# Four edits to a kernel with a planned order: idle products between the first sums, a split first piece, high words first, remainder first

## The chip, the cores and the metric

The kernel runs on one NeuronCore of a Trainium2 chip. The metric is device time in microseconds of one execution. The engines of the core are named PE (TensorE; PEld is its weight load), DVE (VectorE), ACT (ScalarE), POOL (GpSimd) and SP (SyncE, which here issues nearly all transfers). Each engine works through its own list of instructions in the order in which they were written, and an instruction waits for semaphores of the others.

## The reference, cut to what matters

For 2048 positions of 576 channels, a gate mixes two branches:

```python
x = A_u
g = sigmoid((x * gate_w).sum(-1, keepdims=True))
a = _A_ref(x, A_re, A_im, B_re, B_im, C_re, C_im, log_dt, Dskip)   # long convolution
b = _B_ref(x, w_q, k1, k2, u, v)                                   # 4096 experts
return g * a + (1 - g) * b
```

Branch A builds a filter of 2048 taps for each channel, K = Re(sum over 128 states of C exp(dt A l) dt B), and convolves each channel with it (in the reference by FFT); `u * Dskip` is added. Branch B projects every position with `w_q` to 32 heads of two halves, scores each half against 64 keys (`s1 = q1 k1^T`, `s2 = q2 k2^T`), takes the two best of each, the two best of their four sums, a softmax over these two, and forms

```python
act = gelu(einsum("nd,nhkd->nhk", xf, u[top_e]))
out = einsum("nhk,nhk,nhkd->nd", g, act, v[top_e])
```

with `u` and `v` of 4096 rows (the experts).

## The kernel before, in words

**What is multiplied.** No expert row is gathered. All 2048 x 4096 products of positions and expert rows (`a`), all scores against keys folded with `w_q` (`s`), and the output product with a sparse weight matrix (`o`) are dense matmuls. For precision each f32 operand is scaled by a power of two and split into two f16 words, a high one (`hi = f16(s*x)`) and a low one (`s*x - hi`). A product of two operands is then three matmuls: high by high, high by low, low by high. The 576 channels are four pieces of 128 and a remainder of 64, in which high and low word share the 128 rows. `triple` (L943 on) writes one such group: twelve matmuls of 512 columns for the four pieces and two for the remainder (`wrem`).

**Stages.** First the start: the inputs come in, x is read in four blocks of 512 positions (`x_load`, `x_first`, `x_build`), the expert rows u in eight blocks of 512 (`u_load`, `u_build`). For each operand a scale is needed first: ACT squares the values and sums them along the row (`accum_out`, which adds a short ACTIVATION_READ_ACCUMULATOR), PE adds these sums over the partitions with a matrix of ones (`onesb`; bank `sq`), and DVE makes a power of two of the result in four one-column operations (`root_scale`). For the first blocks of x and u, `scale_first` does this in four parts, the remainder and PARTS (two pieces, one, one), as the transfers land, and each part has its own sum matmul of one column into `sq`. `x_norm` forms the squared norms of the 512 positions in a bank `x`; for the first block it first writes six products of 512 columns whose result is not used, waits until u's sums are written, and then writes the five real ones.

The second stage, up to about 678 us, mixes `s` and `a` groups with the making of the filter (`kP`, `kb` matmuls with much work on ACT, DVE and POOL) and the position transform of x, the first stage of the convolution's forward transform (`u_stage1`, bank `u`, 16 steps). The third does the rest of the convolution's transforms (`k`, `pr`/`pi`, `pv`) beside the other `s` groups and the last `a` groups. The last, from about 991 us, takes the 16 tiles of 128 positions one after the other in the sequence ORDER: one-hot matrices that DVE builds by comparison (`onehot`: A, Be, Bg), 256 small one-hot products a tile that scatter the gate weights (bank `S`, in two groups, q = 0 and q = 2), a multiplication on DVE that empties the banks into `gl`, the split into `wh` (high and low words), and then 192 matmuls `o` with the expert rows `v`.

**What sets the order.** The program is generated by Python coroutines. Each engine has a modelled free time, and PE's is the planner's clock: `mm` puts it forward by columns/2400 + 0.003 us for each matmul. A coroutine yields until its inputs are ready by this model (`ready`, with `late` as an extra delay) or a buffer is free (`need`, `take`, `free`), and is called again at that modelled time; the main loop then writes the next `s` or `a` group. What comes out is one fixed order for each engine; on the chip only semaphores hold an instruction back, and one that waits holds all that is behind it on its engine. PSUM has eight banks of [128, 512] f32, given out under quotas (`sc`, `wb`, `kb`).

**Lines that the steps touch.** `mm` L205-L214 (all matmuls carry L214, all DVE, ACT and POOL operations L134, all transfers L205), `squares` L445, `x_norm` L463, `x_first` L481, `scale_first` L503, `u_stage1` L1074, `onehot` L1497, `prep` L1510, `u_load` L1320, `u_build` L1335, and the main loop from L1743. In `u_stage1` a step has two column halves (hh, 288 columns each), two frequency rows (g, on 64 rows of the array each) and three products (z, w): z picks the high or low word of the table `tu`, w that of the data `uh`, whose high word ACT writes and whose low word DVE writes.

Of the kernel before, what the change touches and what calls it, by code (L numbers as in the profile page):

```python
# [17 lines left out]
AF = mybir.ActivationFunctionType  # L18
# [120 lines left out]
def body(ctx: ExitStack, tc: tile.TileContext, xT, au, par, logdt, dskip, gatew, wq, kT, uT, vv,  # L139
# [196 lines left out]
    def newcol(again=False):  # L336

        col[again] += 1
        c = 96 + col[1] % 96 if again else col[0]
        return slice(c, c + 1)  # L340

    def short(c0, n):

        return sc[:, c0:c0 + n].bitcast(BF16)[:, 1:2 * n:2]
# [100 lines left out]
    def squares(a, r, sq, dst):  # L445

        acc = newcol(), newcol()
        S.activation(sq[:, 0:4, :], a, AF.Square, accum_out=sc[:, acc[0]])
        S.activation(sq[:, 4, :], r, AF.Square, accum_out=sc[:, acc[1]])
        yield from ready(sq)  # L450
        tag = side()
        yield from need(tag)
        p = bank(tag, "sq")
        mm(p[:, 0:2], onesb, short(acc[0].start, 2), True, True, 0.05)
        yield from ready(p)
        V.tensor_reduce(out=dst, in_=p[:, 0:2], axis=AX, op=OP.add)
        free(tag, dst)

    marks = {"x": [], "s": [], "h": [], "u": []}
    first_u = [None, None]  # L460
    ahead, normed = [], []

    def x_norm(tb, sq):  # L463

        yield from need("kb")
        p = bank("kb", f"x{tb}")
        if tb == 0:
            for k in range(6):
                mm(p, onesb, sq[:, k % 4, :], True, True)
            while not marks["s"]:  # L470
                yield 0.1
        for k in range(5):
            mm(p, onesb, sq[:, k, :], k == 0, k == 4)
        normed.append(tb)
        yield from ready(p)
        while tb == 0 and 1 not in scaled:
            yield 0.3
        V.tensor_reduce(out=nx[:, tb:tb + 1], in_=p, axis=AX, op=OP.max)
        free("kb", nx)
# [23 lines left out]
    def scale_first(a, r, sq, keep=None):  # L503

        acc = [newcol() for _ in range(1 + len(PARTS))]
        if keep is None:
            V.memset(sq[64:128, 4], 0.0)
        V.memset(sc[64:128, acc[0]], 0.0)
        yield from ready(r)
        S.activation(sq[0:64, 4], r[0:64], AF.Square, accum_out=sc[0:64, acc[0]])  # L510
        V.tensor_copy(r[64:128], r[0:64])
        for n, (m, w) in enumerate(PARTS):
            yield from ready(a[:, m:m + w])
            S.activation(sq[:, m:m + w], a[:, m:m + w], AF.Square, accum_out=sc[:, acc[n + 1]])
        yield from ready(sq)
        yield from need("kb")
        p = bank("kb", "sq")
        for n, c in enumerate(acc):
            mm(p[:, 0:1], onesb, short(c.start, 1), n == 0, n == len(PARTS), 0.05)
        yield from ready(p)  # L520
        out = root_scale(p[:, 0:1], 1.02)
        if keep is not None:
            V.tensor_copy(keep, p[:, 0:1])
        free("kb", out[0])
        return out
# [548 lines left out]
    def u_stage1():  # L1074
        nonlocal uf
        yield from need("slot")
        us = slot([4, D], F32, "us")
        columns.add(us.tensor.name)
        s_u, i_u = root_scale(nx2, 1.02)
        ended = [0]  # L1080
        ld = {}

        def load(p):
            a = us[:, p % 2, :]
            for g in range(2):
                l, far = U_PAIRS[2 * p + g]
                dma(a[64 * g:64 * g + 64], bass.AP(tensor=au.tensor, offset=au.offset + l * D,
                                                   ap=[[64 * D, R1], [(far - l) * D, 2], [1, D]]))
            tu = uf.tile([128, 2, 128], F16, tag="tu", name=f"tu{p}", bufs=2)
            dma(tu, tu_d[:, p])  # L1090
            ld[p] = a, tu

        def tail(p, tag, pbs):
            for g in range(2):
                o = us[:, 2 + g, :]
                for hh in range(2):
                    pb = pbs[hh][g]
                    yield from ready(pb)
                    ov = o[:, 288 * hh:288 * hh + 288]
                    S.activation(ov, pb[:, :288], AF.Copy)  # L1100
                    free(tag, ov)
                yield from ready(ov)
                dma(pair_rows(su_d, 2 * p + g), o)
            ended[0] += 1

        load(0)
        for p in range(NT):
            a, tu = ld.pop(p)
            yield from ready(a, tu)
            while ended[0] < p - 1:  # L1110
                yield 0.3
            h = uf.tile([128, 2, D], F16, tag="uh", name=f"uh{p}", bufs=2)
            S.activation(h[:, 0], a, AF.Copy, scale=s_u)
            yield from ready(h)
            V.scalar_tensor_tensor(h[:, 1], a, s_u, h[:, 0], op0=OP.mult, op1=OP.subtract)
            if p + 1 < NT:
                load(p + 1)
            yield from ready(h)
            while ended[0] < p:
                yield 0.3  # L1120
            tag = side()
            hungry[0] = p * NCK < 17 * kdone[0]
            yield from need(tag, 4)
            hungry[0] = False
            pbs = [[bank(tag, f"u1_{p}_{g}_{hh}") for g in range(2)] for hh in range(2)]
            for hh in range(2):
                cs = slice(288 * hh, 288 * hh + 288)
                for n, (z, w) in enumerate(((0, 0), (0, 1), (1, 0))):
                    for g in range(2):
                        r = slice(64 * g, 64 * g + 64)  # L1130
                        mm(pbs[hh][g][:, :288], tu[r, z], h[r, w, cs], n == 0, n == 2, 0.063)
            spawn(tail(p, tag, pbs))
            del pbs
            yield 12
        while ended[0] < NT:
            yield 1
        free("slot")
        quota(raw=2)
        while not kstored[0]:
            yield 1  # L1140
        V.scalar_tensor_tensor(iuk, iuk, 2.0 ** -28, i_u, op0=OP.mult, op1=OP.mult)
        UF.__exit__(None, None, None)
        uf = 0
# [176 lines left out]
    def u_load(c):  # L1320
        a = slot([4, 512], F32, f"us{c}")
        r = actp.tile([128, 512], F32, tag="ur", name=f"ur{c}")
        cs = slice(512 * c, 512 * c + 512)
        if c:
            dma(a, uT[0:512, cs].rearrange("(k p) n -> p k n", p=128))
        dma(r[0:64], uT[512:576, cs])
        if c:
            dma(r[64:128], uT[512:576, cs])
        else:
            halves_load(a, uT, cs)  # L1330
        return a, r
# [3 lines left out]
    def u_build(c):  # L1335
# [23 lines left out]
        rem = wrems[c % 2]  # L1359
        if c == 0:  # L1360
            for k in range(4):
                S.activation(hl[:, 0, k, :], a[:, k, :], AF.Copy, scale=s)
                marks["h"].append(S.free + 0.28)
            S.activation(rem[:, 0, :], r, AF.Copy, scale=s)
            marks["h"].append(S.free + 0.28)
# [144 lines left out]
    def prep(t):  # L1510
# [17 lines left out]
                yield 0.3  # L1528
            oh = {q: onehot(t, q) for q in range(3)}
        for q in (0, 2):  # L1530
            yield from ready(*oh[q], *oh[q + 1], late=2.5 if t in ORDER[:3] else 0.0)
            yield from need("wb", 4)
            pbs = []
            for d in (q, q + 1):
                A, Bg = oh.pop(d)
                both = [bank("wb", f"S{t}_{d}_{r}") for r in range(2)]
                for j in range(16):
                    for z in range(2):
                        for r, pS in enumerate(both):
                            rows = slice(64 * r, 64 * r + 64)  # L1540
                            mm(pS[:, 32 * j:32 * j + 32], A[rows, j // 2, :, j % 2], Bg[rows, z, j // 2, :, j % 2],
                               z == 0, z == 1, 0.014)
                pbs.append((16 * d, both))
                del both, pS
            if q == 0:
                oh[3] = onehot(t, 3)
            for n0, both in pbs:
                for r, pS in enumerate(both):
                    yield from ready(pS)
                    pv = pS.rearrange("p (k b) -> p b k", b=32)  # L1550
                    for h in range(2):
                        gv = gl[h].rearrange("p b (r n) -> p b r n", r=2)[:, :, r, n0:n0 + 16]
                        V.tensor_tensor(out=gv, in0=pv[:, 16 * h:16 * h + 16], in1=gv, op=OP.mult)
                    free("wb", *gl)
            del pbs, pS, pv, both
# [311 lines left out]
```

## Time and profile before

| | |
|---|---|
| median of 3 runs | 1441.61 us |
| lowest, highest | 1441.29, 1444.52 us |
| profiled execution, its time | 1442.26 us |
| profiled execution, span from first to last instruction | 1440.3 us |
| PE busy | 1421.2 us (99%) |
| DVE, ACT, POOL busy | 1161.8, 769.9, 484.2 us |
| granted TensorE clock | 1.000 |
| matmuls | 16151 |

The profile is one execution on the chip. Busy time is time in which at least one instruction of the engine was under way; matmuls are pipelined, so a train of them is shorter than the sum of their durations: a 512-column matmul shows 379 ns in a train, and twelve of them take 2.75 us. In the timeline each row has a start (us from the span's start), a duration, the engine, the operation and its tiles as output<-inputs, and in brackets the idle time before it and what ended it; neighbouring instructions of a kind are merged into one row with their count. In the list of waits a row names the waiting engine and tile, what it waited for, the total, the number of times and the longest. SPq is SP's queue of transfers.

### The profile page before, as it was taken

To read this page: it belongs to the slowest core of one execution; us is meant where nothing else is said; L and a number is where in the kernel's file an instruction comes from. 1 tells how busy PE (TensorE), PEld (TensorE's weight loads), DVE (VectorE), ACT (ScalarE), POOL (GpSimd) and SP (SyncE) were. 2 spreads that over 40 slices of the span, in tenths; PEclk is the share of its full clock that TensorE was granted. 3 is DMA by queue.
4 is the path that set the end of the run, shared out by engine and by line. 5 is a ranking of instruction groups with operands and counts; after the bars stand their busy time and mean duration, and the time that the engine had idled before them with its cause. 6 is when DMAs were issued, how large, how long until landed. Compare 5 with 4: busy or idle time off the path is not lost.

```text
span 1440.3 us, 40769 instructions
## 1 busy us (share of the span) xinstructions
PE 1421.2 (99%) x16151; PEld 835.6 (58%) x16153; DVE 1161.8 (81%) x4595; ACT 769.9 (53%) x1281; POOL 484.2 (34%) x492
## 2 busy tenths in 40 slices
PE   7999999999999999999999999999999999999999
PEld 3444445455455445455555444456787787787785
DVE  6899899879886997875999897689877777877840
ACT  6346876796784876844655655666333223323310
POOL 0325357547356346230547899700000000000000
PEclk9999999999999999999999999999999999999999
DMA  8235323442334323159675677967443332442400
GB/s 302 75 116 165 90 74 121 126 144 72 109 100 154 93 93 115 49 172 308 222 264 191 243 258 271 307 216 249 151 131 130 117 122 95 136 147 69 159 10 17
DMA packets 134239, 215.43 MB, mean 150 GB/s; under 512 B 11040, under 2 KB 79904, under 8 KB 127648
## 3 DMA queue, kind: packets, MB, share of 16 engines
q1 hardware_dynamic: 133952, 212.80, 45.2%
q8 instruction: 127, 2.08, 0.6%
q14 instruction: 64, 0.52, 0.1%
q10 hardware_dynamic: 96, 0.02, 0.0%
HBM read 141.48 MB, written 71.30 MB: 148 GB/s over the span
## 4 chain that ended last, share of the span: by engine, by line
PE 87%; DVE 5%; DMA 1%; issue 0%; ACT 0%; SPq 0%; DVEq 0%
PE o L214 25%; PE s L214 24%; PE a L214 21%; PE S L214 3%; PE kb L214 2%; PE pr L214 2%; PE wb L214 2%; PE pv L214 1%; PE y L214 1%; PE kP L214 1%; PE k L214 1%; PE u L214 1%; DVE vhl L134 1%; DMA wq<-in_wq_dram 1%; DVE gl L134 1%; DVE A L134 1%
## 5 line engine op out<-in xcount | busy, mean ns | idle before, releaser
L214 PE MATMUL o<-vhl,wh 128*128 128x288 f16 (+2 forms) x3072 | 382.7, 286 | 0.0
L214 PE MATMUL s<-whl,xb 128*128 128x512 f16 x1536 | 363.9, 379 | 0.0
L214 PE MATMUL a<-xb,uhl 128*128 128x512 f16 x1536 | 358.8, 379 | 0.5 <-ACT uhl L134 0.3
L214 PEld LDWEIGHTS <-wh 128*128 128x128 f16 x3072 | 292.4, 98 | 84.1 <-issue 3.7
L214 PEld LDWEIGHTS <-xb 128*128 128x128 f16 x1792 | 170.7, 98 | 209.2 <-issue 14.5
L214 PEld LDWEIGHTS <-uhl 128*128 128x128 f16 x1536 | 147.3, 98 | 177.4 <-issue 3.2
L134 DVE FIND_INDEX8 i<-m,s 128x8 uint32<-128x64 f32 x1024 | 206.1, 219 | 0.0
L134 ACT ACTIVATE wh<-gl,s_wg 128x1024 f16<-128x1024 f32 x64 | 69.0, 1137 | 197.5 <-DVE gl L134 197.5
L134 DVE MAX8 m<-s 128x8 f32<-128x64 f32 x1024 | 145.9, 212 | 30.4 <-PE s L214 29.4
L134 POOL TENSOR_TENSOR CS<-CS,ex 128x512 f32<-128x512 f32 x72 | 98.0, 1392 | 147.5 <-DVE ex L134 146.1
L134 DVE TENSOR_TENSOR gl<-S,gl 128x256 f32<-128x256 f32 x256 | 88.4, 413 | 36.8 <-PE S L214 36.8
L134 ACT ACTIVATE go<-a,i_a 128x512 f32<-128x512 f32 x93 | 62.5, 684 | 97.2 <-PE a L214 70.2
L134 POOL TENSOR_TENSOR e<-aN,rt 128x512 f32<-128x512 f32 x72 | 83.2, 1176 | 49.9 <-PE kb L214 43.8
L134 DVE TENSOR_TENSOR A<-iota_a,vals 128x2048 f16<-128x2048 f16 x64 | 77.9, 1217 | 23.3 <-PE S L214 23.3
L134 ACT ACTIVATE gl<-gl 128x1024 f32<-128x1024 f32 x64 | 63.6, 1045 | 45.3 <-DMA gl<-g_d 36.8
L134 DVE SCALAR_TENSOR_TENSOR wh<-gl,s_wg,wh 128x1024 f16<-128x1024 f32 x62 | 77.6, 1279 | 12.4 <-ACT wh L134 12.3
L214 PE MATMUL s<-wrem,xb 128*128 128x512 f16 x256 | 76.2, 379 | 0.0
L214 PE MATMUL a<-xb,wrem 128*128 128x512 f16 x256 | 75.9, 379 | 0.0
L134 DVE MATCH_VALUE_LOAD i<-m,s 128x8 f32 x1024 | 69.4, 68 | 0.1
L134 ACT ACTIVATE CS<-CS 128x1024 f32<-128x1024 f32 x57 | 59.2, 1044 | 7.3 <-DVE CS L134 7.3
L134 POOL TENSOR_TENSOR ex<-ex,gN 128x512 f32<-128x512 f32 x36 | 44.8, 1256 | 53.3 <-ACT ex L134 53.1
L134 DVE SCALAR_TENSOR_TENSOR ya<-o,om,ya 128x288 f32<-128x288 f32 (+2 forms) x32 | 15.1, 512 | 55.4 <-PE o L214 55.4
(209 smaller groups left out, 2098.3 us busy)
## 6 DMA issues: line engine op xcount, KB each, us to landing
g_d<-go SPq DMA_DIRECT2D x128, 256.0 KB, 2.5
gl<-g_d SPq DMA_DIRECT2D x32, 1024.0 KB, 5.5
wq<-in_wq_dram SPq DMA_DIRECT2D x16, 1152.0 KB, 5.6
su_d<-us SPq DMA_DIRECT2D x32, 288.0 KB, 2.6
sk_d<-k1o SPq DMA_DIRECT2D x32, 288.0 KB, 2.7
ui<-su_d SPq DMA_DIRECT2D x16, 576.0 KB, 3.9
ki<-sk_d SPq DMA_DIRECT2D x16, 576.0 KB, 5.5
vn<-in_vv_dram SPq DMA_DIRECT2D x32, 288.0 KB, 5.4
```

The costliest lines, as they stand in the source:

```text
L134: return f(*a, **k)
L214: T.matmul(o, l, r, start=start, stop=stop)
```

## The change

In the start, `scale_first` takes the bank `x0` itself and writes products of 512 columns whose result is not used between its one-column sums: for x four on the remainder's squares ahead of the second sum, one ahead of the third, one ahead of the fourth; for u two ahead of the third sum and one ahead of the fourth, all on x's squares. The six in `x_norm` stay. The first piece of the first expert rows' high words is made by ACT (256 columns) and DVE (256 columns) instead of ACT alone. In the position transform all products with high data words come first, over both column halves, and those with the low words last. For the second and later blocks of expert rows, the two remainder loads are issued before the large load, and the remainder's square is written before the large square. For the first three tiles the one-hot products are written when their matrices are 3.8 us old by the planner's clock, not 2.5.

```diff
     def squares(a, r, sq, dst):
         acc = newcol(), newcol()
+        S.activation(sq[:, 4, :], r, AF.Square, accum_out=sc[:, acc[1]])
         S.activation(sq[:, 0:4, :], a, AF.Square, accum_out=sc[:, acc[0]])
-        S.activation(sq[:, 4, :], r, AF.Square, accum_out=sc[:, acc[1]])
...
+    first_x = []
...
     def x_norm(tb, sq):
-        yield from need("kb")
-        p = bank("kb", f"x{tb}")
+        if tb:
+            yield from need("kb")
+        p = bank("kb", f"x{tb}") if tb else first_x[1]
...
         p = bank("kb", "sq")
+        if keep is None:
+            yield from need("kb")
+            first_x.extend((sq, bank("kb", "x0")))
+        idle_on, over = first_x
+        idle_at = ((), (4,) * 4, (0,), (2,)) if keep is None else ((), (), (0, 1), (2,))
         for n, c in enumerate(acc):
+            for k in idle_at[n]:
+                mm(over, onesb, idle_on[:, k], True, True)
             mm(p[:, 0:1], onesb, short(c.start, 1), n == 0, n == len(PARTS), 0.05)
...
-            for hh in range(2):
-                cs = slice(288 * hh, 288 * hh + 288)
-                for n, (z, w) in enumerate(((0, 0), (0, 1), (1, 0))):
+            for n, (z, w) in enumerate(((0, 0), (1, 0), (0, 1))):
+                for hh in range(2):
+                    cs = slice(288 * hh, 288 * hh + 288)
                     for g in range(2):
                         r = slice(64 * g, 64 * g + 64)
                         mm(pbs[hh][g][:, :288], tu[r, z], h[r, w, cs], n == 0, n == 2, 0.063)
...
-        if c:
-            dma(a, uT[0:512, cs].rearrange("(k p) n -> p k n", p=128))
         dma(r[0:64], uT[512:576, cs])
         if c:
             dma(r[64:128], uT[512:576, cs])
+            dma(a, uT[0:512, cs].rearrange("(k p) n -> p k n", p=128))
         else:
             halves_load(a, uT, cs)
...
             for k in range(4):
-                S.activation(hl[:, 0, k, :], a[:, k, :], AF.Copy, scale=s)
+                w = 512 if k else 256
+                S.activation(hl[:, 0, k, :w], a[:, k, :w], AF.Copy, scale=s)
+                if k == 0:
+                    V.tensor_scalar(hl[:, 0, k, w:], a[:, k, w:], s, None, op0=OP.mult)
                 marks["h"].append(S.free + 0.28)
...
         for q in (0, 2):
-            yield from ready(*oh[q], *oh[q + 1], late=2.5 if t in ORDER[:3] else 0.0)
+            yield from ready(*oh[q], *oh[q + 1], late=3.8 if t in ORDER[:3] else 0.0)
```

## The prediction, made before the result was known

> **What bounds the kernel now.** First the page: the busy shares say which engine the time belongs to.
>
> ```profile
> PE 1421.2 (99%) x16151; PEld 835.6 (58%) x16153; DVE 1161.8 (81%) x4595; ACT 769.9 (53%) x1281; POOL 484.2 (34%) x492
> ```
>
> PE is busy for 1421.2 of the span's 1440.3 us, so only 19.1 us are left in which it has nothing in flight. No other engine can become the bound by a few instructions; an edit is worth something only if it shortens one of PE's waits or adds one. So the second view is the list of what PE waited for, and here it is over the whole span.
>
> ```profile
> PE sq L214 <- ACT xb L134: 8.7, 4, 4.6
> PE u L214 <- DVE uh L134: 2.0, 2, 1.4
> PE kb L214 <- issue: 1.5, 1, 1.5
> PE sq L214 <- ACT uhl L134: 1.4, 2, 1.0
> PE S L214 <- DVE gl L134: 0.7, 2, 0.5
> PE k L214 <- DMA ksb<-k_d: 0.6, 1, 0.6
> ```
>
> The columns are the total, the number of times and the longest. The first row is the start, before any input has arrived. The second is the position transform, the fourth the sums of the expert rows, the fifth the one-hot products: one edit of the change lies at each of them. I went to each in the timeline, the third view, first to the start (start, duration, engine; times are from the span's start).
>
> ```profile
> 4.56 0.16 PE L214 MATMUL sq<-sc,onesb 128*128 128x1 bf16 x1 [4.56 <-ACT xb L134]
> 7.48 0.16 PE L214 MATMUL sq<-sc,onesb 128*128 128x1 bf16 x1 [2.76 <-ACT xb L134]
> 8.09 0.16 PE L214 MATMUL sq<-sc,onesb 128*128 128x1 bf16 x1 [0.45 <-ACT xb L134]
> 9.22 0.16 PE L214 MATMUL sq<-sc,onesb 128*128 128x1 bf16 x1 [0.97 <-ACT xb L134]
> 9.25 2.72 PE L214 MATMUL x<-xb,onesb 128*128 128x512 bf16 x6
> 11.76 0.39 PE L214 MATMUL sq<-sc,onesb 128*128 128x1 bf16 x3
> 12.60 0.16 PE L214 MATMUL sq<-sc,onesb 128*128 128x1 bf16 x1 [0.45 <-ACT uhl L134]
> 12.63 1.24 PE L214 MATMUL x<-xb,onesb 128*128 128x512 bf16 x5
> 14.21 2.76 PE L214 MATMUL a<-xb,uhl 128*128 128x512 f16 x12 [0.35 <-ACT uhl L134]
> ```
>
> These are PE's rows alone. ACT's and DVE's in the same stretch that the edit touches:
>
> ```profile
> 10.18 1.06 ACT L134 ACTIVATE uhl<-us 128x1024 bf16<-128x1024 f32 x1 [0.39 <-DMA us<-in_uT_dram]
> ...
> 11.23 0.61 ACT L134 ACTIVATE uhl<-us 128x512 bf16<-128x512 f32 x1
> ...
> 13.31 0.15 DVE L134 COPY nu<-sq 128x1 f32<-128x1 f32 x1
> 13.38 0.47 DVE L134 TENSOR_SCALAR xb<-xs,sci 128x512 f16<-128x512 f32 x1
> 13.44 2.56 ACT L134 ACTIVATE uhl<-us,sci 128x512 f16<-128x512 f32 x4 [0.89 <-DVE sci L134]
> ```
>
> Up to 12.60 the sums wait for squares, and the squares for inputs. From the last sum the path is: scale on DVE, first high words on ACT, first real product at 14.21. From there PE runs with hardly a gap, so whatever this point moves, the end moves by.
>
> **First high words on two engines.** ACT now makes 256 of the first piece's 512 columns and DVE the rest. Between 1024 and 512 columns ACT's time falls from 1.06 to 0.61, 0.45 for 512 columns, so half a piece saves 0.22 us. DVE's half lies between its 1-column copy (0.15) and its 512-column scaling (0.47); I take the middle, 0.31, so from 13.46 it ends at 13.77, before ACT's half at about 13.92. The first two products read ACT's half, the next two DVE's. The five x products ahead of them, at some 0.22 from 12.63 on, leave the array free from about 13.7. So the first product comes at 13.99: **-0.22 us** (ends 0, if the array is not free, and -0.5, if only those five bound it). DVE's 0.31 pushes all its later work in the start. The cover: the pieces of x it delays come after 16 products of about 0.23 us (2.76 for 12), some 3.7 us. Without that cover it would cost 0.31.
>
> **Idle products.** Nine more products of 512 columns: four, one and one between the four sums of x, two and one between those of u; the six that stood behind x's sums stay. The six took 2.72 us, some 0.42 each after allowing for the longer last one; the five at 12.63 took 1.24, about 0.22 each. So the array doubled its pace somewhere between. At 0.42 each, the four in x's sums take 1.7 us of a gap of 2.76, and the single ones 0.42 of 0.45 and of 0.97: they fit. In u's sums, the three at 0.22 each end at about 12.5, before ACT releases the last sum at 12.60: nothing. At 0.42 each they end at about 13.1 and hold that sum back by 0.48 us. The array has had work since 4.56 by then, much more than before, and had the 0.22 us pace at 12.63 without it; I take **0**, and keep +0.48. There is no gain either: the first real products already ran at 0.23 us each.
>
> [...]
>
> **High words first in the position transform.** The products come in pairs on two halves of the rows.
>
> ```profile
> 96.00 0.30 PE L214 MATMUL u<-uh,tu 64*128 64x288 f16 x2
> 96.91 0.79 PE L214 MATMUL u<-uh,tu 64*128 64x288 f16 x10 [0.62 <-DVE uh L134]
> ...
> 115.22 0.30 PE L214 MATMUL u<-uh,tu 64*128 64x288 f16 x2
> 116.94 0.79 PE L214 MATMUL u<-uh,tu 64*128 64x288 f16 x10 [1.42 <-DVE uh L134]
> ```
>
> One pair runs, then PE waits until DVE has written the low words (`uh`), then ten run. Ten take 0.79 with a last one of 0.30, so a pair costs (0.79 - 0.30)/4 = 0.12. In the new order four pairs need no low words, three more than now: 3 x 0.12 = 0.37 of each wait is filled. Two waits: **-0.73 us** (ends: 0, if the planner puts these steps where DVE is not late, and -0.73). The banks of the first half finish up to 0.25 us later, so ACT's copies do too; they feed a store, and nothing on PE waits for that. No instruction is added.
>
> **Remainder first.** For the second and later expert rows the two remainder loads and their square go ahead of the large one.
>
> ```profile
> 72.62 0.67 SPq L205 DMA_DIRECT2D us<-in_uT_dram  x1
> 73.34 1.50 SPq L205 DMA_DIRECT2D ur<-in_uT_dram  x2
> ...
> 79.18 1.91 ACT L134 ACTIVATE uhl<-us 128x2048 bf16<-128x2048 f32 x1 [2.11 <-DMA us<-in_uT_dram]
> ...
> 81.85 0.16 PE L214 MATMUL sq<-sc,onesb 128*128 128x2 bf16 x1 [0.95 <-ACT uhl L134]
> ...
> DMA to landing us min/median/max: 5.8/6.1/6.3
> ```
>
> The last row is that of the remainder's loads in this stretch. ACT waits for the large load (79.18), squares it, then the remainder (0.61, as the same shape took at 11.23), then the sum can run, 2.67 us after the landing. With the remainder done in ACT's idle time this would be 2.06. But the second remainder load was issued at about 74.25 and landed near 80.05, right behind the large one: they land in order of issue. Put last, the large load lands near 80.05, and the sum runs at 82.1 instead of 81.85: **+0.2 us**. If the large load landed when it does now, it would be 0.6 sooner; if the issue of two more loads ahead of it also leaves the wire idle for as long as they take on it (80.05 - 79.18 = 0.87), 1.1 later. On SP the three issues take as long in either order, so nothing behind them is held. For the six later expert rows the list of PE's waits has no entry: nothing.
>
> **Later one-hot products.** For the first three tiles they are emitted 1.3 us later on the planner's clock.
>
> ```profile
> 996.26 1.77 PE L214 MATMUL S<-Bg,A 64*128 64x32 f16 x128
> ...
> 1006.88 0.97 PE L214 MATMUL S<-Bg,A 64*128 64x32 f16 x64
> 1007.29 1.41 DVE L134 TENSOR_TENSOR gl<-S,gl 128x256 f32<-128x256 f32 x4
> ...
> 1008.10 0.19 PE L214 MATMUL S<-Bg,A 64*128 64x32 f16 x1 [0.25 <-DVE gl L134]
> ...
> 1008.76 0.96 PE L214 MATMUL S<-Bg,A 64*128 64x32 f16 x63 [0.47 <-DVE gl L134]
> ```
>
> The third tile's second group takes 2.84 us from first to last (1006.88 to 1009.72) where the one before takes 1.77: 1.07 lost while DVE, four evictions from 1007.29 to 1008.70, gives back banks. Started 1.3 later, at 1008.2, its first half ends at 1009.1, behind the last eviction: **-1.07 us** (ends -1.07 and 0). PE has other products to run meanwhile. Queued behind those groups are DVE's evictions and splits, which the output products of the tile read; the list of PE's waits has no row for output products, so this is covered now, and would cost up to 1.3 a group if it were not.
>
> **The sum** is -0.22 + 0 - 0.73 + 0.2 - 1.07 = -1.8 us. The profiled execution took 1442.26 us (span 1440.3, 2.0 around it), 0.65 above the median of 1441.61. So the sum gives 1440.4 for such an execution and **1439.8** as a median. All good ends together give -2.9 (1438.7), all bad ones (0.48 and 1.1) +1.6 (1443.2).
>
> **The rivals.** What the parts do not hold is the order. The planner counts 0.216 us for each 512-column product, so nine of them put its clock forward by about 2 us in the start, where the chip has idle time. Everything planned behind it, the mixture of a, s and kb products above all, falls out somewhat differently.
>
> *The redrawn order gives the gain back* (0.27). The waits above are accidents of one order: two out of sixteen transform steps, one sum out of seven. Another order can have as many elsewhere; one new wait like the 1.5 of kb or the 1.42 at 116.94 takes most of the sum, two take all. Time 1441.6, with one more such wait 1443.1. Against it: the one-hot wait lies among output products, behind the mixture, where little is left to be redrawn.
>
> *It removes others too* (0.12). Without the waits of kb (1.5), sq (1.0 more) and k (0.6), 3.1 us more go: 1436.7. Nothing in the edits aims at them.
>
> *The array keeps its 0.42 us pace through u's sums* (0.07): if work in bursts with pauses of 0.5 to 1 us between them does not bring the 0.22 us pace by 12.6, the idle products cost their 0.48, and the gain is 1.3: 1440.3. Against it: in this execution the pace had changed by 12.63 with less work before it. [...]
>
> *Slower: the hand-over at 650 to 680 runs dry* (0.09). There PE lives on products of the expert rows while the filter's last blocks are written and read back.
>
> ```profile
> 652.16 2.75 PE L214 MATMUL a<-xb,uhl 128*128 128x512 f16 x12
> ...
> 679.11 1.39 PE L214 MATMUL k<-ksb,tk 128*128 128x288 f16 x10 [0.58 <-DMA ksb<-k_d]
> ```
>
> The cover was already 0.58 us short. A group is these twelve products and two remainders, fourteen at 0.216 (2.75 for twelve with a longer last one) or 3.0 us. Each group that the new order spends earlier is missing here and exposes 3.0 us of the transfer. One group undoes the gain and more: 1442.8; two make 1445.9. It decides from 1.8 us on. Against it: the reserve is counted by the same planner, and only one wait of 0.6 is there now.
>
> **How the numbers follow.** The forecast, 1439.8, has 0.45, with 1438.7 to 1441.0 as its own range. About 0.3% (4.3 us) can be told from no change: faster is below 1437.3, slower above 1445.9. Faster is the third case and a sliver, 0.13; slower half of the hand-over, 0.05; same 0.82. The range runs from 1436.4, which takes in the removal of other waits, to 1443.8, which takes in one new wait (1443.1) and one missing group (1442.8) with the 0.65 by which the two executions above differ.
>
> **What would show it.** Right: the first a product near 14.0, with two x products between the sums of u; six to eight u products before a wait for uh instead of two; no S wait near 1008; the large load of the second row landing behind the remainder. Wrong: the last sum of u after 12.7; a first product at 14.2 or later; a wait of PE of over 1.5 us where there was none, above all ahead of the output products; PE's busy time, 1421.2, up by more than the nine products (about 3 us).

## The result, and the profile after

The changed kernel took 1454.36 us (median of 6 runs, 1452.22 to 1455.87) against 1443.43 us (6 runs, 1441.29 to 1444.52) for the kernel before on the same chip: ratio 1.0077, with a 95% interval from 1.0067 to 1.0088. It is 11 us slower; the forecast was 1439.8, with 1443.8 as the upper end of the range. The profiled execution took 1453.11 us, with a span of 1451.2 and a mean granted clock of 0.996 instead of 1.000.

The page's row of the engines, and then the list of PE's waits:

```profile
PE 1428.3 (98%) x16159; PEld 837.7 (58%) x16162; DVE 1168.5 (81%) x4607; ACT 767.8 (53%) x1276; POOL 471.8 (33%) x485
```

```profile
PE sq L214 <- ACT xb L134: 5.8, 3, 4.4
PE wn L214 <- ACT wj L134: 3.1, 5, 1.1
PE tr L214 <- ACT go L134: 3.0, 1, 3.0
PE a L214 <- DVE vals L134: 2.9, 1, 2.9
PE a L214 <- DVE i L134: 1.5, 1, 1.5
PE u L214 <- DVE uh L134: 1.2, 2, 1.0
PE sq L214 <- ACT uhl L134: 1.1, 1, 1.1
```

The rows that the change aimed at did shrink (`u` from 2.0 to 1.2, `S` and `kb` gone), but four rows are new: `wn`, `tr`, `a <- vals`, `a <- i`, 10.5 us together. And PE is busy for 7.1 us more, of which nine products of 0.22 to 0.42 us explain at most 3.8; the rest is slower work. By stage: the first `a` product comes 0.30 us sooner (13.91 for 14.21), from there to the first output product it takes 988.96 us for 976.8, and the last stage, to the end of the last output product, 445.0 for 446.0. The loss lies in the middle, and most of it in one place. PE there, in the timeline:

```profile
937.47 0.33 PE L214 MATMUL tr<-identb,vals 128*64 128x64 bf16 x4 [2.95 <-ACT go L134]
...
941.36 5.28 PE L214 MATMUL a<-xb,uhl 128*128 128x512 f16 x12 [2.91 <-DVE vals L134]
946.43 1.04 PE L214 MATMUL a<-xb,wrem 128*128 128x512 f16 x2
947.28 2.77 PE L214 MATMUL a<-xb,uhl 128*128 128x512 f16 x12
```

`tr` are the transposes that bring the experts' positions into the order of the one-hot matrices; ACT and DVE copy them out as `vals`. Two waits of 2.9 us, and then twelve products take 5.28 us where the next twelve take 2.77. The same stretch in windows of 5 us (PE, PEld, DVE, ACT and POOL busy with their counts, then the granted clock, the transfers' share of the engines and GB/s):

```profile
930.00:935.00 5.00, 4.52 (x92) 3.24 (x90) 0.00 (x0) 4.97 (x8) 0.00 (x0) 1.00 1.05 392
935.00:940.00 5.00, 0.97 (x16) 0.89 (x16) 0.00 (x0) 5.00 (x9) 0.00 (x0) 0.71 1.03 368
940.00:945.00 5.00, 3.64 (x9) 1.28 (x9) 4.26 (x11) 0.30 (x1) 0.00 (x0) 0.50 0.07 20
945.00:950.00 5.00, 5.00 (x19) 2.03 (x18) 4.93 (x13) 2.01 (x3) 0.00 (x0) 0.77 0.17 47
```

DVE does nothing for ten microseconds, and the transfers take 1.05 and 1.03 of the engines' time. The granted clock is about half from 937 to 947: it is 1.00 from 936 to 937, 0.54 in the next microsecond, 0.50 from 938 to 947, and 0.84 from 947 to 948, so it fell at the end of the first wait, before the second. That makes 5.9 us of waits and about 3 us of half clock (5.28 - 2.77 for the twelve, 1.04 - 0.59 for the two remainders). The two waits have two causes. The first ends with ACT's `go`, and ACT is not idle then: it has just loaded a table (1.28 us) and worked through four `gl`, which in the kernel before were done at 934.25.

```profile
932.95 3.90 ACT L134 ACTIVATE gl<-gl 128x1024 f32<-128x1024 f32 x4
936.75 0.67 ACT L134 ACTIVATE go<-a,i_a 128x512 f32<-128x512 f32 x1
```

The second ends with DVE's `vals`. What DVE waits for stands in its own row, and SP's queue shows why:

```profile
940.71 0.29 DVE L134 CAST iota_a<-cst 128x256 f16<-128x256 f32 x1 [14.08 <-DMA g_d<-go]
```

```profile
925.16 2.74 SPq L205 DMA_DIRECT2D vhl<-in_vv_dram  x2
928.00 1.31 SPq L205 DMA_DIRECT2D z_d<-vo  x1
```

`iota_a` lies in memory that the transforms' tiles give back, and the program makes its copy wait until the last of their stores, `z_d` from the last `vo`, has landed. The store is issued at 928.00, behind two loads of 1152 KB each, and lands 12.4 us later, at 940.4. (The row names `g_d`, the transfer that came last by the profile.) The copies of `vals` stand behind `iota_a` on DVE. In the kernel before, the store is issued ahead of these loads, and `iota_a` follows after 2.62 us:

```profile
927.41 0.33 SPq L205 DMA_DIRECT2D z_d<-vo  x1
...
931.17 1.24 SPq L205 DMA_DIRECT2D vhl<-in_vv_dram  x2
```

```profile
931.30 0.29 DVE L134 CAST iota_a<-cst 128x256 f16<-128x256 f32 x1 [2.62 <-DMA g_d<-go]
```

### The profile page after: what moved, and what is told of

It is laid out like the page before. It is cut to its first block, busy times and chain, and to the rows that moved or that the text cites. A ratio compares the mean times of both kernels' runs of the same rounds, so it can differ in the third digit from the quotient of the medians.

```text
span 1451.2 us, 40804 instructions
## 1 busy us (share of the span) xinstructions
PE 1428.3 (98%) x16159; PEld 837.7 (58%) x16162; DVE 1168.5 (81%) x4607; ACT 767.8 (53%) x1276; POOL 471.8 (33%) x485
## 4 chain that ended last, share of the span: by engine, by line
PE 87%; DVE 4%; DMA 1%; ACT 1%; SPq 0%; issue 0%; POOL 0%; ACTq 0%; DVEq 0%; POOLq 0%
PE o L214 26%; PE a L214 23%; PE s L214 22%; PE S L214 4%; PE pr L214 2%; PE kb L214 2%; PE wb L214 2%; PE pv L214 1%; PE y L214 1%; PE kP L214 1%; DVE i L134 1%; PE u L214 1%; DVE m L134 1%; PE k L214 1%; DMA wq<-in_wq_dram 1%; DVE e L134 0%
## 5 line engine op out<-in xcount | busy, mean ns | idle before, releaser
L214 PE MATMUL a<-xb,uhl 128*128 128x512 f16 x1536 | 362.7, 381 | 4.8 <-DVE vals L134 2.9
```

The source lines that it names most:

```text
L214: T.matmul(o, l, r, start=start, stop=stop)
```

## The experiments

**What redraws the order.** The instruction lists can be compared without a run. The idle products alone change 26 lines of PE's list, all where they stand; the split piece none; the later one-hot products move one group by six output products. High words first, alone, moves about 2000 of PE's instructions and over 300 of DVE's, and gives the changed kernel's order but for the other edits' own instructions. The edit issues no further instruction; but the four banks of a step are complete at other times by the planner's clock (0.06 to 0.25 us), and everything behind them is fitted in anew. Remainder first alone also redraws it (over a thousand of PE's instructions).

**All five edits in the old order** (`e1_order_kept`): the instructions are the changed kernel's, but the planner is given the old times.

```
+mm(over, onesb, idle_on[:, k], True, True, 0.0)
+rdy[key(pbs[hh][g])] = clock[0] - 0.063 * (7 - 6 * hh - g) + 0.4   # u banks, as in the old order
...
+(remainder loads first, with queue, wire and ready times of the old order)
+(first piece: DVE's half without its model time, ACT's free time as for 512 columns)
```

> All five edits, but the planner's clock and ready times are kept as they were before the change: the idle products count nothing, DVE's half piece counts as ACT's, the u banks and the three loads get the times of the old order. So every engine's order is that of before but for the edits themselves. Theory A (the loss comes from the order that the planner redrew, above all from the hand-over near 930 us): 1.0 to 2.5 us less than before, ratio 0.9982 to 0.9993, no new wait of PE. Theory B (the edited instructions cost the time themselves): about 11 us more, ratio 1.006 to 1.009.

Measured: 1439.65 us (1438.28 to 1441.04), ratio 0.9978 (0.9969 to 0.9987). Its waits:

```profile
PE sq L214 <- ACT uhl L134: 1.9, 1, 1.9
PE u L214 <- DVE uh L134: 1.0, 1, 1.0
PE S L214 <- DVE gl L134: 0.8, 2, 0.5
```

None of the four new rows is there. The edits themselves are worth about 3 us; the redrawn order costs some 14. The `sq` row grew by more than the 0.2 of the prediction, and the `S` row stayed, against it. The sums show how the loads land:

```profile
74.50 0.54 SPq L1347 DMA_DIRECT2D us<-in_uT_dram  x1
...
81.05 1.91 ACT L134 ACTIVATE uhl<-us 128x2048 bf16<-128x2048 f32 x1 [3.03 <-DMA us<-in_uT_dram]
```

The large load, issued last, lands 6.5 us after its issue, as long as when it was first (72.62 to 79.18).

**Only the ready times of high words first** (`e2_u_times_only`): the kernel before, not one instruction edited, but the banks' times of the new order are told to the planner.

```
+rdy[key(pbs[hh][g])] = clock[0] - 0.063 * (3 - 2 * hh - g) + 0.4
```

> No edit at all in the instructions: the u products stand in the old sequence, but the planner is given the ready times of their banks that the new sequence would give (the first column half 0.25 us later, the second 0.06 to 0.13). Theory A: the order is redrawn as in the changed kernel, and the time is 10 to 13 us more than before, ratio 1.007 to 1.009, with PE's two waits of about 3 us near 935. Theory B: as before, ratio 0.999 to 1.001.

Measured: 1460.56 us (1459.1 to 1462.1), ratio 1.012 (1.0104 to 1.0135). A shift of at most 0.25 us in a model costs 17 us on the chip. Its waits are of the same kinds (and it has waits by "issue" besides, 1.8 us on `kb` and 3.0 on `S` and `o`):

```profile
PE a L214 <- DVE vals L134: 3.3, 1, 3.3
PE wn L214 <- ACT wj L134: 3.3, 4, 1.1
PE tr L214 <- ACT go L134: 2.9, 1, 2.9
```

**The last store first** (`e3_z_store_first`): the changed kernel, with the loads of rows v held until the last `z_d` store is issued.

```
+    z_out.append(k)                       # at each z_d store
-while not vnormed or c not in vt ...
+while not vnormed or 15 not in z_out or c not in vt ...
```

> The changed kernel, but the first loads of the rows v wait in the program until the last z store has been issued, so that this store stands ahead of them on SP. Theory A: the store lands some 7 to 8 us sooner, DVE's wait ahead of iota_a shrinks from 14 us to under 6, PE's two waits near 935 (5.9 us) and the half clock behind them (3 us) go: 8 to 9.5 us less than the changed kernel, ratio to before 1.001 to 1.0025. Rival C (the loss is spread over many small new waits, and the hand-over costs only its own 5.9 us or less): ratio to before 1.0035 to 1.007.

Measured: 1447.03 us (1445.79 to 1449.74), ratio 1.003 (1.0019 to 1.004), some 7 us below the changed kernel; 8 to 9.5 had been expected, and DVE's wait ahead of `iota_a` shrinks to 8.12, not to under 6. The place, in the timeline and in windows:

```profile
935.76 0.31 PE L214 MATMUL tr<-identb,vals 128*64 128x64 bf16 x4 [0.88 <-DVE vals L134]
```

```profile
935.00:940.00 5.00, 4.24 (x33) 2.24 (x33) 4.85 (x12) 5.00 (x10) 0.00 (x0) 1.00 1.06 377
```

One wait of 0.88 is left of 5.9, and the clock stays at 1.00. The second train of twelve begins 7.9 us sooner than in the changed kernel's trace (939.43 for 947.28), and the span is 6.6 us shorter. The store still takes 7.9 us to land (issued 927.0); two 1024 KB loads of `gl` stand ahead of it and the loads of v right behind, and which of them holds it is not shown. Not all of the gain is the store's: every engine but SP works in the changed kernel's order, but in the built program the last `tr` group of this place has another PSUM bank, and so it runs at 935.76, ahead of ACT's `go` at 937.12, on which it waited before. The share of each is not separated.

**All but high words first** (`e4_all_but_u`), the changed kernel with the old loops in the transform:

```
-for n, (z, w) in enumerate(((0, 0), (1, 0), (0, 1))):
-    for hh in range(2):
+for hh in range(2):
+    for n, (z, w) in enumerate(((0, 0), (0, 1), (1, 0))):
```

> The changed kernel without the edit of the u products. Theory A: the order is another one again (the loads put the other way round redraw it too), without the changed kernel's hand-over: within 4 us of before, ratio 0.997 to 1.003. Theory B with the cost in the idle products, the split piece, the loads or the one-hot products: ratio 1.006 to 1.009.

Measured: 1439.6 us (1438.91 to 1441.09), ratio 0.9973 (0.9964 to 0.9982). This order too is redrawn, by the remainder loads, yet it has neither the `tr` nor the `vals` wait. Not every redraw is bad; the one that this edit sets off is.

**The mirror: v loads first in the kernel before** (`e5_v_loads_first`).

```
+    if k == 15:
+        for c0 in (0, 1):
+            v_load(c0)
     dma(freq_rows(z_d, k) ...
```

> The kernel before with one thing changed at the hand-over: the first two loads of the rows v are issued just ahead of the last z store instead of behind it (the order of what follows shifts a little). Theory A (that pair is the cause): the last z store lands 6 to 8 us later, DVE's wait ahead of iota_a grows from 2.6 to 8 to 14 us, PE waits 3 to 6 us near 935, with or without a spell of half clock: 4 to 9 us more than before, ratio 1.003 to 1.0065. Rival D (the store's place only hurts together with the rest of the changed order): ratio 0.999 to 1.0015.

Measured: 1452.42 us (1449.93 to 1453.98), ratio 1.005 (1.0031 to 1.0069). The wait is made where there was none:

```profile
PE tr L214 <- DVE vals L134: 5.4, 1, 5.4
```

The store, issued at 924.37 behind the loads, lands 13.3 us later, and DVE's wait ahead of `iota_a` is 12.88 us for 2.62. So a store put behind these loads makes DVE's wait and PE's behind it. The rest of the order is not quite that of before, though (some hundreds of PE's instructions change places), and of the 8 us about 4 lie in the last stage, behind waits by "issue" of 0.5 to 2.0 us.

**Idle products in the two waits** (`e6_idle_in_gap`): the changed kernel, with 44 products of 128 columns whose result is not used in each wait, so that the array has work.

```
+if t in (8, 12):
+    for n in range(44):
+        mm(both[n % 2][:, 384:512], onesb, onesb, True, True, 0.0)
```

> The changed kernel in its own order, with 44 products of 128 columns whose result is not used in each of PE's two waits near 935, written to unused columns, 2.5 us each, counted as nothing by the planner. If the half pace behind the waits (12 a products in 5.28 us) comes from PE's being idle: the clock stays at 1.00, they take 2.75 us, and 2.5 to 3.5 us of the changed kernel's 11 go, ratio to before 1.0045 to 1.006. If it comes from something else at that place (transfers, banks): no change, ratio 1.007 to 1.0085.

Measured: 1456.61 us (1454.22 to 1457.93), ratio 1.0083 (1.0066 to 1.01): the time expected did not come. In the trace the clock part did, with a granted clock of 1.00 in every window of 5 us from 925 to 955:

```profile
941.54 2.75 PE L214 MATMUL a<-xb,uhl 128*128 128x512 f16 x12 [0.63 <-DVE vals L134]
```

From first `a` to first `o` it is 3.2 us shorter than the changed kernel; but the last stage is 6.0 us longer, with a row that PE had not had there:

```profile
PE o L214 <- issue: 4.4, 3, 2.6
```

"issue" means that the profile shows nothing that PE waited for. Behind the longest of these waits (2.55 us) the granted clock fell again, to 0.60 and 0.54 in the two windows of 2 us from 1010 to 1014.

**Order kept, without remainder and one-hot edit** (`e7_order_kept_three`), the run `e1_order_kept` with these two undone:

```
-dma(r[0:64] ...); dma(r[64:128] ...); dma(a ...)   # and the remainder's square first
+dma(a ...); dma(r[0:64] ...); dma(r[64:128] ...)
-late=3.8
+late=2.5
```

> As the first experiment (order of before kept), but only with three edits: idle products, split piece, high words first; the loads and squares of the remainder and the delay of the one-hot products are as before. If the remainder's edit costs (its sum waited 1.89 us against 0.95 in the profile of before) and the delay brings nothing: 0.5 to 1.2 us less than the first experiment, ratio to before 0.9968 to 0.9976. If one of the two edits helps somewhere else: as the first experiment or above, 0.9977 to 0.999.

Measured: 1442.45 us (1441.72 to 1444.66), ratio 0.999 (0.9979 to 1.0001), outside the range expected of the prediction's terms and at the end of the other. The `kb <- issue` wait near 453 is back (2.1 us). It had been in every profile with the old order of loads and in none with the remainder first, and that led to the next run.

**Remainder first for one block only** (`e8_one_row_remainder_first`): three loads near 447 us in another order, nothing else.

```
-dma(a ...); dma(r[0:64] ...); dma(r[64:128] ...)
+if c == 5: dma(r[0:64] ...); dma(r[64:128] ...); dma(a ...)   # planner's times as before
```

> The kernel before with one edit at one place: for the sixth expert rows alone (the loads issued at 447.5 us) the two remainder loads are issued ahead of the large one; every engine's order but SP's three issues is as before. Theory (the order of these three issues decides PE's wait of 1.5 to 2.1 us among the kb products near 453): no kb row in the list of waits, the sum wait near 82 us as before (0.95), and 1.5 us less, ratio 0.9985 to 0.9995. Rival (the wait comes and goes by something else that the order-kept kernels share): the kb row is there with 1.5 to 2.1 us, ratio 0.9997 to 1.0003.

Measured: 1441.35 us (1438.98 to 1442.71), ratio 0.9984 (0.9976 to 0.9993), a little more than expected, and no `kb` wait. The transfers' view says what the 1.35 us by which the large load is later do. In the kernel before, from 452.3 to 454 us (queue: packets, MB, share):

```profile
q1 hardware_dynamic: 565, 0.46, 90.4%
q8 instruction: 1, 0.02, 4.1%
```

There is no such packet from 447 to 452.3; there the transfers of data, the large load among them, take 92.1% of the engines' time (101.9% from 450 to 452.3). In the run with the other order it falls between 450 and 452.3:

```profile
q1 hardware_dynamic: 631, 0.52, 86.1%
q8 instruction: 1, 0.02, 2.9%
```

Queue q8, on the page an instruction queue, brings PE's by the count: 127 packets of 16 KB for 32,304 matmuls and weight loads, one for every 254; with PE's own waits the trace holds 32,466, 256 a packet or an estimated 64 bytes each. In the trace the packet begins at 452.58 and takes 1.11 us; PE stops at 453.8 and goes on at 455.32, 1.6 us after it has landed. The other order lets it begin at 451.70, and PE does not stop. All fourteen traces agree: in the six with the large load first here, the packet begins 0.5 to 1.0 us behind the first of these `kb` products, and PE waits 1.2 to 2.1 us; in the other eight it begins 1.7 to 2.6 us ahead of them, and PE does not wait. That it is the instructions, the count shows: all 21 waits by "issue" of over 0.23 us that PE has behind the start in the fourteen traces end 1.3 to 1.6 us behind the landing of such a packet, and at one place of the list, 190 to 195 PE instructions (matmuls, weight loads and PE's own waits) above a multiple of 256. The kernel before has two of them: 1.50 us here, with the 1 MB load issued 5.1 us ahead of the packet and PE in a block of short matmuls (eight `kb` products in 0.29 us), and 0.25 us at 1239.75.

**High words first alone, in the old order** (`e9_high_first_alone`), the kernel before with the new loops and the old times:

```
+for n, (z, w) in enumerate(((0, 0), (1, 0), (0, 1))):
+    for hh in range(2):
...
+rdy[key(pbs[hh][g])] = clock[0] - 0.063 * (7 - 6 * hh - g) + 0.4
```

> High words first in the position transform alone, with the planner's times, and so the order of all engines, as before. If the edit is worth what the prediction's term says, the two u waits shrink by 0.37 each (to about 0.2 and 1.0) and the time by 0.7 us, ratio 0.9990 to 1.0000; the kb wait near 453 (1.5 to 2.1) and the S waits near 1006 (0.25 and 0.47) stay. Rival (the products after the wait take up what it gives): u waits shorter, but the time from the first u product of a step to the last as before.

Measured: 1442.01 us (1440.51 to 1446.02), ratio 0.9993 (0.9984 to 1.0002). The first step runs through without a wait, the second waits 1.05 for 1.42.

**Later one-hot products alone** (`e10_late_alone`), `late=3.8` for 2.5:

> The later one-hot products alone, with the planner's own order (two dozen rows of PE differ). Prediction's term: no S wait near 1006, and 1.07 us less, ratio 0.9990 to 0.9996. Rival, as seen in the order-kept kernel: the groups only move by six output products, both S waits stay (0.25 to 0.3 and 0.47), ratio 0.9997 to 1.0003. The kb wait near 453 stays in both cases (1.5 to 2.1).

Measured: 1443.27 us (1441.42 to 1445.4), ratio 0.9997 (0.9987 to 1.0007). The rival held:

```profile
996.70 1.77 PE L214 MATMUL S<-Bg,A 64*128 64x32 f16 x128
...
1007.83 0.19 PE L214 MATMUL S<-Bg,A 64*128 64x32 f16 x1 [0.27 <-DVE gl L134]
1008.49 0.96 PE L214 MATMUL S<-Bg,A 64*128 64x32 f16 x63 [0.47 <-DVE gl L134]
```

The first group moved six output products later, the second stayed behind the same output product (72 products between the two in before, 66 here). So the age of its one-hot matrices is not what sets its place; by the code that leaves `need("wb", 4)`, the banks. Both waits end with DVE's evictions, and these stand behind 8.4 us of DVE's other work without a gap (998.61 to 1007.02).

**The rest of the edits, old order, second rows as before** (`e11_order_kept_rest`), the run `e1_order_kept` with:

```
-if c: (remainder loads first)
+if c > 1: (remainder loads first)
-(remainder's square first; late=3.8)
+(large square first; late=2.5)
```

> Order as before, with the idle products, the split first piece, high words first, and remainder loads first for the third and later expert rows only (the second as before); squares and one-hot products as before. Theory: start 0.2 less, u waits 0.7 less, kb wait gone (1.5 to 2.1 less), sum wait of the second rows about 0.95 as before: 2.4 to 3.0 us less, ratio 0.9970 to 0.9985, so 0.5 to 1 us below the kernel with all five edits in the old order (0.9978). Rival (the kb wait hangs on something else): it stays, ratio 0.9987 to 0.9997.

Measured: 1439.78 us (1438.52 to 1440.46), ratio 0.9975 (0.9966 to 0.9984), within the expectation; against `e1_order_kept` (0.9978) no difference can be told. It and the runs `e1_order_kept` and `e4_all_but_u` beat both kernels.

**A whole packet of idle instructions** (`e12_idle_256`): 64 products of 96 columns in each of the two waits of the changed kernel, 256 instructions in all.

```
+if t in (8, 12):
+    for n in range(64):
+        mm(both[n % 2][:, 416:512], onesb, onesb[:, 0:96], True, True, 0.0)
```

> The changed kernel with 64 idle products of 96 columns in each of the two waits near 935 and 938, so 256 instructions more on PE (128 weight loads and 128 matmuls) instead of the 176 of the run with 44 in each; the packets that bring PE's instructions hold 16 KB, and 256 instructions of 64 bytes fill one. Theory (the o waits of that run, 4.4 us by no work that the profile shows, came from where a refill fell, and the clock theory was right): with a whole packet more, the refills behind the waits fall where they fell in the changed kernel, so no o wait by issue over 1 us, an o stage of about 445 us, the first a train behind the second wait at 2.75 us, and about 3 us less than the changed kernel (1.0077): ratio 1.0045 to 1.0065. Rival (idle products bring the o waits whatever their number): o waits by issue of 3 to 5 us again and a ratio of 1.007 to 1.009.

Measured: 1453.12 us (1449.71 to 1457.11), ratio 1.0067 (1.0049 to 1.0085). The long `o` waits are gone, as by the theory:

```profile
PE wn L214 <- ACT wj L134: 3.6, 3, 1.4
...
PE o L214 <- issue: 1.0, 3, 0.5
```

A group of 128 one-hot products and its weight loads is about one packet of instructions, and PE runs it in 1.77 us. In `e6_idle_in_gap` such a group starts at 1006.10, a packet begins at 1008.00, and PE stops for 2.55 us behind the group. In this run a packet begins just as far into that group (1.95 us for 1.90), and PE does not stop; what differs is where in the list the group lies, by 80 instructions against the multiples of 256. That this place decides is argued from the two outcomes, not shown by itself. The train behind the second wait takes 2.75 us and PE gains 3.0 us there, but the time comes out above what was expected, though its interval reaches into the expected ratios. In the profiled execution the clock halved elsewhere, behind two `wn` waits of 1.40 and 1.12:

```profile
690.00:692.00 2.00, 2.00 (x40) 1.90 (x36) 0.00 (x0) 0.00 (x0) 0.00 (x0) 0.50 0.96 372
```

In the changed kernel, with 0.19 and 1.12 there, it did not; in `e2_u_times_only`, with 1.03 and 1.12, it did (0.50 from 692 to 694).

## Why the prediction was wrong, point by point

- **The order, the step that failed.** The sum held nothing for it, and the rival "the redrawn order gives the gain back" sized it as one or two waits of 1.5 us out of those that the trace of before showed. The runs show some 14 us: the same edits give 0.9978 in the old order and 1.0077 in the new one. Two assumptions in it fell. Its cause was put down to the nine idle products; it is high words first, a few tenths of a microsecond in the banks' ready times (`e2_u_times_only`, 1.012 with no instruction edited). And new waits were sized by the old ones, while the worst stood where before had none: two waits of 2.9 us, one behind ACT's `gl` and one behind DVE's `iota_a`, and 3 us of half clock, at a place where a 2.62 us wait of DVE was covered. The row that warned of the second was there to be read: `z_d` ahead of `vhl` on SP by 3.8 us, with `iota_a` and `vals` queued behind the store's landing. About 7 of the 11 us go in the run that puts that store first, in which ACT's wait goes too; `wn` and `a <- i` (4.6) are the main rows of the rest, and what brings them was not followed up.
- **The slower rival** named the hand-over at 650 to 680. The wait of 0.58 there is gone in the changed kernel. What came, 270 us later, is like it only in that a transfer landed later than the work at hand could cover: not `a` groups spent too early, but a store behind two loads, and ACT's order.
- **High words first, -0.73.** The two steps themselves are as sized: from the first product of a step to the last it takes 1.24 and 2.13 us in the changed kernel for 1.70 and 2.51 before, 0.84 less. Alone in the old order (`e9_high_first_alone`) the median fits too, but its interval takes in no change.

```profile
95.80 0.66 PE L214 MATMUL u<-uh,tu 64*128 64x288 f16 x8
96.62 0.42 PE L214 MATMUL u<-uh,tu 64*128 64x288 f16 x4 [0.15 <-DVE uh L134]
...
114.56 0.66 PE L214 MATMUL u<-uh,tu 64*128 64x288 f16 x8
116.27 0.42 PE L214 MATMUL u<-uh,tu 64*128 64x288 f16 x4 [1.05 <-DVE uh L134]
```

- **First high words, -0.22.** From the last sum to the first `a` product it is 1.43 us (12.48 to 13.91) for 1.61: -0.18. Over all traces it is 1.43 to 1.76 us with the edit and 1.61 to 2.11 without, and there the pace of PE has a part, as follows.
- **Idle products, 0 (end +0.48).** In the profiled pair 0, as forecast. Over all traces neither. The last sum of u does come some 0.47 us later in six of the eight executions with the new start (3.87 to 3.88 us after the six `x` products begin; 3.28 to 3.50 in all others), which was the end and the third rival. But the pace of the start, which was read from one execution, differs from one to the next. Here is that of `e8_one_row_remainder_first`, whose start is the old one:

```profile
12.63 0.16 PE L214 MATMUL sq<-sc,onesb 128*128 128x1 bf16 x1 [0.45 <-ACT uhl L134]
12.66 2.29 PE L214 MATMUL x<-xb,onesb 128*128 128x512 bf16 x5
```

  The five products that took 1.24 us in before take 2.29. From the six `x` products to the product behind the first twelve `a` products, six executions with the old start take 7.61 to 9.60 us (mean 8.54), eight with the new one 7.36 to 8.23 (mean 7.91). So the start gains about 0.6 us on average, and the execution that the prediction quoted was the quickest of the old ones. Its 0 rested on that one; the sentence that there is no gain either is not borne out by the mean. The five products behind the last sum take 1.24 to 1.85 us in the eight and 1.24 to 2.30 in the six. Whether the idle products do this or chance, no run here settles by time, and what sets the pace is not shown.
- **Remainder first, +0.2.** At the sum it is +0.95 in the old order (1.9 for 0.95), near the bad end of 1.1: the loads do not land one behind the other at the same last time; the large one is later by what the two issues ahead of it take, 1.60 us (72.90 to 74.50), and lands 6.5 us behind its own issue as it did before. What the prediction put at nothing, the six later rows, brought the gain: the `kb` wait of 1.2 to 2.1 us goes, by PE's instructions.
- **Later one-hot products, -1.07.** 0 in the old order: the edit does not move the group it was costed on, as the code's `need("wb", 4)` could have told.

## What to carry to other kernels

Where a program's order comes from a planner, an edit's first price is what it does to the planner's times: compare the two instruction lists before costing anything, and keep the old order while the edit itself is tried. Give each new wait its own releaser: two that stood side by side here had two causes. Then look in the new order for transfers that have changed places in a queue, above all a store whose landing frees memory for the next stage, and follow who is queued behind it. A wait with no releaser in a train of short matmuls can be the instruction supply, as the `kb` waits of 1.2 to 2.1 us were here: look at the packets of the instruction queue and at the large load ahead of them.

## What the runs showed of the hardware that was not expected

PE's instructions come by transfers of a queue of their own, which the page counts on the same 16 engines as the data: 127 packets of 16 KB, 0.6% of the engines' time. A packet that came late, behind a 1 MB load, went with a stop of PE of 1.2 to 2.1 us in six traces; 176 more instructions ahead of a dense group of one-hot products went with waits of up to 2.6 us at one place (`e6_idle_in_gap`), 256 with none over 0.5 (`e12_idle_256`). The 21 stops of over 0.23 us all lie 190 to 195 PE instructions above a multiple of 256. So semaphores are not all that held an instruction back here.

The granted clock fell behind short waits too. In the changed kernel it was 0.54 in the microsecond in which a wait of 2.95 us ended, and 1.00 again from 948, eleven microseconds later; behind one of 2.55 us in `e6_idle_in_gap` it was 0.60 and 0.54 (the windows of 2 us from 1010 to 1014), and behind one of 2.0 in `e5_v_loads_first` 0.66 and 0.50 (those from 1072 to 1076). Two waits of 1.40 and 1.12, parted by one product of 0.16 us, stood ahead of 0.50 in `e12_idle_256`, and 1.03 and 1.12 ahead of 0.50 in `e2_u_times_only`; 1.30 and 1.12 at the same place (`e3_z_store_first`) left it at 1.00. Behind the single `kb` waits of 1.2 to 2.1 us nine `a` products took 2.12 us in all six traces, no longer than elsewhere. Which waits bring the lower clock the runs do not settle. In the changed kernel it cost about 3 us.
